# Attention with rotary embedding and a gated block: transposes whose result nobody reads, kept only ahead of the first rotary sum

## Chip, cores and metric

One core of a Trainium2 chip runs the whole program. The metric is device time in microseconds (us) of one execution, the median over several. The engines are TensorE (PE, with its weight loads PEld beside it), VectorE (DVE), ScalarE (ACT), GpSimd (POOL) and SyncE (SP), which issues DMAs. The matrix results of PE go to PSUM banks, from which DVE and ACT read.

## What is computed

Eight batches of eight heads, 576 positions, head width 64. Queries and keys are rotated, attention is computed, and the heads of one batch together (512 wide) go through a causal convolution of five taps, a sigmoid gate and two 512 x 512 products:

```python
q_rot, k_rot = rotate(q), rotate(k)
scores = (1 / sqrt(D)) * q_rot @ k_rot.T
attn = exp(scores - max(scores)); attn /= sum(attn) + 1e-9
x = heads side by side of (attn @ v)          # B, S, 512
gate = sigmoid(sum over k of conv_w[k] * x shifted by k)
out = (gate * (x @ w_val)) @ w_out
```

## The kernel before

Work goes in 32 pairs of heads (`p`), four pairs to a batch. For a pair the queries fall into four chunks of 128 positions and a fifth that holds the last 64 positions of both heads. The steps that matter here, with their lines:

- `rope_mul`, `rope_add` (L283, L287) rotate; for pair 0 alone `rope_mm` (L294) makes the rotary sum on PE. `qk_hi`, `qk_lo` (L303 to L314) split each value into a high and a low part.
- `s_mm` (L339), a **score chunk**: 12 matmuls for the two heads of a chunk (6 for the fifth), each head into a score bank `ps_s`. There are two such banks.
- `s_max` (L345), the **row maximum**, on DVE; `s_exp` (L353), the exp, on ACT, which also hands over the row sums (the READ_ACCUMULATOR rows). Only then is the score bank free for the next chunk.
- `t_mm` (L400, L365), a **turn**: PE transposes the exp results into banks `ps_t`, of which there are four; `t_copy` (L438, L440) copies them to SBUF.
- `pv_mm`, `pv_left` (L449, L459) multiply with the values; `x_norm` (L506) divides by the sums, `tap` (L532) and `gate` follow.
- `f_mm` (L572): the two 512-wide products of a batch, in 24 groups of matmuls for each stage, between the pairs of the next batch. Until 96 us there is none of this work yet to put between.

Every engine takes its instructions in the order in which the program issues them. That order is not found by rules: the string `ORDER` lists all jobs one by one, with the buffers that each takes, and `Plan.run` walks through it. A second table, `FILLS`, maps a position in this list to a pair of numbers (count, bank). When the walk comes to such a position, `fill` (L356) first issues that many transposes of the identity matrix into the `ps_t` bank named, ahead of the job. Nothing reads what they write:

```python
def fill(n, slot):
    bank = psum.tile([128, 512], F32, name="ps_t", tag=f"ps_t{slot}")
    for _ in range(n):
        T.transpose(out=bank[:, 0:128], in_=ident, identity=ident)
```

They read only `ident`, but they take a `ps_t` bank like any job, so they wait for whoever had it last, and the next job that takes it stands behind them. They appear in the trace as L360. The first group of 34, at position 11, stands ahead of `rope_mm`, while PE has no data. The next ten stand at these places: 21, 26 and 11 transposes between the score chunks and turns of pair 0; 7 ahead of the fifth chunk of pair 1; 2 ahead of the second chunk of pair 2; 5 between pairs 2 and 3; 13 between pairs 3 and 4 and 3 behind the first chunk of pair 4; 3 and 7 around the fifth chunk of a later pair, at 137 and 139 us.

Of the kernel before, what the change touches and what calls it, by code (L numbers as in the profile page):

```python
# [161 lines left out]
3252 3268 3261 3253 3262 3275 3254:2 3284:2 3250 3255 3285 3256 3276 3286 3277V:0 3289:1 3278 3287A:2 3290 3294:0 3291 3304:3 3292V:1 3295 3293 3299:2  # L162
3288 3300 3301 3296 3302V:0 3305 3303 3297A:1 3306 3298 3307A:2 3308
"""
FILLS = {11: (34, 0), 46: (21, 0), 63: (26, 2), 90: (11, 3), 176: (7, 0), 207: (2, 2), 277: (5, 1), 360: (13, 2), 372: (3, 3), 647: (3, 3), 660: (7, 2)}


class Plan:
# [16 lines left out]
    def run(self, engine, fill, behind):  # L185
# [10 lines left out]
        for step, entry in enumerate(ORDER.split()):  # L196
# [4 lines left out]
            writer.update(dict.fromkeys(w, i))  # L201
            if step in FILLS:
                fill(*FILLS[step])
            self.slots = [int(x) for x in slots]
# [691 lines left out]
```

## Time and profile before

| what | before |
|---|---|
| median of three runs | 674.58 us (674.34 to 674.8) |
| the profiled execution: its time | 675.45 us |
| its span, first to last instruction | 673.7 us |
| mean granted PE clock in it | 0.997 |
| DVE busy, ACT busy, POOL busy | 553.5 (82%), 514.2 (76%), 288.9 us (43%) |
| L360 MATMUL, the filling transposes | 132, 270 to 477 ns each |

Busy time is the time in which an engine had at least one instruction under way; matmuls overlap, so a group's elapsed time is shorter than the sum of its instructions. In the page's rows of slices each digit is the busy share of a fortieth of the span in tenths, and PEclk is the clock that PE was granted, in tenths of full speed. In a row such as `x12 [1.41 <-ACT p L353]` the bracket gives the idle time of the engine just ahead of it and what ended it. Times in timelines count from the start of the span.

### The profile page before, as it was taken

To read this page: it belongs to the slowest core of one execution; us is meant where nothing else is said; L and a number is where in the kernel's file an instruction comes from. 1 tells how busy PE (TensorE), PEld (TensorE's weight loads), DVE (VectorE), ACT (ScalarE), POOL (GpSimd) and SP (SyncE) were. 2 spreads that over 40 slices of the span, in tenths; PEclk is the share of its full clock that TensorE was granted. 3 is DMA by queue.
4 is the path that set the end of the run, shared out by engine and by line. 5 is a ranking of instruction groups with operands and counts; after the bars stand their busy time and mean duration, and the time that the engine had idled before them with its cause. 6 is when DMAs were issued, how large, how long until landed. Compare 5 with 4: busy or idle time off the path is not lost. (4 is left out here: it accounts for less than half of the span.)

```text
span 673.7 us, 18254 instructions
## 1 busy us (share of the span) xinstructions
PE 658.8 (98%) x7224; PEld 534.8 (79%) x7224; DVE 553.5 (82%) x932; ACT 514.2 (76%) x1251; POOL 288.9 (43%) x258
## 2 busy tenths in 40 slices
PE   8889899999999999999999999999999999999998
PEld 7666677778788778887877888877788878787887
DVE  5999899999788888988787988987878889887732
ACT  3989888888887868887777887787778777776722
POOL 0445334423645622253554335456546563353122
PEclk9999899999999999999999999999999999999999
DMA  6435324523422534232434323343433144301112
GB/s 205 141 120 162 118 79 141 170 84 98 152 84 91 165 100 135 75 112 84 139 90 140 105 77 113 96 133 108 134 123 97 47 134 126 99 28 48 35 55 72
DMA packets 46743, 72.66 MB, mean 108 GB/s; under 512 B 15897, under 2 KB 25666, under 8 KB 46658
## 3 DMA queue, kind: packets, MB, share of 16 engines
q1 hardware_dynamic: 46114, 70.91, 34.0%
q8 instruction: 57, 0.93, 0.6%
q10 hardware_dynamic: 544, 0.59, 0.3%
q14 instruction: 28, 0.23, 0.1%
HBM read 61.89 MB, written 9.59 MB: 106 GB/s over the span
## 5 line engine op out<-in xcount | busy, mean ns | idle before, releaser
L345 DVE TENSOR_REDUCE nm<-ps_s 128x1 f32<-128x576 f32 x288 | 207.4, 752 | 58.8 <-PE ps_s L339 56.8
L353 ACT ACTIVATE p<-ps_s,nm 128x576 f32<-128x576 f32 x288 | 213.1, 744 | 54.4 <-DVE nm L345 50.3
L339 PE MATMUL ps_s<-k,q 64*128 64x288 f32 (+1 forms) x1728 | 175.9, 308 | 6.2 <-ACT p L353 5.9
L339 PEld LDWEIGHTS ps_s<-k,q 64*128 64x128 f32 (+1 forms) x1728 | 138.3, 185 | 33.7 <-ACT p L353 19.5
L438 ACT COPY pt<-ps_t 128x512 f32<-128x512 f32 (+1 forms) x241 | 126.7, 547 | 48.2 <-PE ps_t L400 47.2
L449 PE MATMUL ps_a<-pt,v 128*64 128x320 f32 (+1 forms) x1024 | 137.8, 412 | 0.9 <-ACT pt L438 0.4
L400 PEld LDWEIGHTS ps_t<-ident,p 64*128 64x128 f32 x2428 | 99.2, 138 | 21.3 <-issue 8.4
L400 PE MATMUL ps_t<-ident,p 64*128 64x64 f32 x2428 | 110.9, 226 | 1.7 <-ACT pr L438 0.5
L532 DVE SCALAR_TENSOR_TENSOR g<-x,cw,g 128x576 f32<-128x576 f32 (+1 forms) x132 | 108.8, 829 | 2.0 <-ACT g L529 1.5
L572 PE MATMUL ps_f<-y,wout_hi 128*128 128x288 f32 (+2 forms) x512 | 107.1, 302 | 0.4 <-DVE o L596 0.4
L449 PEld LDWEIGHTS ps_a<-pt,v 128*64 128x64 f32 x1024 | 68.0, 136 | 45.8 <-issue 3.1
L572 PEld LDWEIGHTS ps_f<-y,wout_hi 128*128 128x128 f32 x512 | 81.3, 188 | 6.0 <-ACT pt L438 2.1
L283 POOL TENSOR_TENSOR qin<-qin,tab 128x640 f32<-128x640 f32 x39 | 60.3, 1559 | 43.2 <-DVE kin L287 16.6
L572 PE MATMUL ps_f<-xh,wval_hi 128*128 128x288 f32 (+2 forms) x256 | 78.2, 309 | 0.6 <-ACT pt L438 0.3
L572 PE MATMUL ps_f<-xh,wval_lo 128*128 128x288 f32 (+2 forms) x256 | 75.4, 298 | 0.0
L572 PE MATMUL ps_f<-xl,wval_hi 128*128 128x288 f32 (+2 forms) x256 | 75.1, 295 | 0.0
L283 POOL TENSOR_TENSOR kin<-kin,tab 128x576 f32<-128x576 f32 x31 | 43.8, 1418 | 71.2 <-DVE g L532 41.6
L572 PE MATMUL ps_f<-y,wout_lo 128*128 128x288 f32 (+2 forms) x256 | 74.2, 295 | 0.0
L587 POOL TENSOR_TENSOR y<-y,y 128x288 fp32r<-128x288 f32 (+2 forms) x64 | 51.1, 806 | 51.4 <-ACT y L584 23.1
L519 POOL TENSOR_TENSOR xl<-x,xh 128x576 fp32r<-128x576 f32 (+2 forms) x33 | 46.3, 1406 | 55.4 <-ACT xh L513 23.6
L353 ACT ACTIVATION_READ_ACCUMULATOR p<-ps_s,nm 128x1 f32 x288 | 57.5, 200 | 0.0
L572 PEld LDWEIGHTS ps_f<-xh,wval_hi 128*128 128x128 f32 x256 | 47.9, 188 | 7.2 <-ACT pt L438 4.9
(90 smaller groups left out, 841.5 us busy)
## 6 DMA issues: line engine op xcount, KB each, us to landing
kin<-in_k SPq DMA_DIRECT2D x31, 576.0 KB
qin<-in_q SPq DMA_DIRECT2D x31, 512.0 KB
v<-in_v SPq DMA_DIRECT2D x32, 320.0 KB
out_t<-o SPq DMA_DIRECT2D x56, 144.0 KB
rb<-rd SPq DMA_DIRECT2D x31, 144.0 KB
rb<-rd SPq DMA_DIRECT2D x31, 128.0 KB
wst<-in_w_val SPq DMA_DIRECT2D x4, 512.0 KB
wst<-in_w_out SPq DMA_DIRECT2D x4, 512.0 KB
```

The costliest lines, as they stand in the source:

```text
L283: return eng.tensor_tensor(out=t[:, i, a:b], in0=t[:, 0 if p < RAW else i, a:b], in1=table[:, i, a:b], op=ALU.mult)
L339: T.matmul(out=tiles[h][:, half, 0:288], lhsT=st["q"][rows, x, c * 128:c * 128 + 128], rhs=st["k"][rows, y, k0:k0 + 288], start=(i == 0), ...
L345: V.tensor_reduce(out=st[f"nm{i}"], in_=st[f"s{i}"], axis=AX.XY, op=ALU.max, negate=True)
L353: A.activation(out=st[f"p{t}"][:, part].rearrange("p (b x) -> p b x", b=2), in_=st[f"s{i}"], func=AF.Exp, bias=st[f"nm{i}"], scale=1.0, ac ...
L400: T.transpose(out=st["b" + key + x][:, k * D:(k + 1) * D], in_=src[rows], identity=ident[rows, rows])
L438: A.copy(out=dst, in_=src)
L449: T.matmul(out=st[f"a{g}"][HEAD[h], 0:n], lhsT=st["v"][:, j, h, :], rhs=st[f"pt{g}"][:, h * 4 + j], start=(j == 0), stop=False)
L519: return G.tensor_tensor(out=st["xl"][:, a:b], in0=xs[p % 2][:, 4 + a:4 + b], in1=st["xh"][:, a:b].bitcast(F32), op=ALU.subtract)
L532: return V.scalar_tensor_tensor(out=g, in0=x_sb[:, a + k:b + k], scalar=w, in1=g, op0=ALU.mult, op1=ALU.add)
L572: T.matmul(out=acc[:, 0:n], lhsT=wt[w][:, kc, ds], rhs=mv, start=(kc == 0 and i == 0), stop=(kc == NCH - 1 and i == 2))
L587: return G.tensor_tensor(out=ffn[b][1][:, dc, lo:hi], in0=ffn[b, "y", dc, lo], in1=ffn[b][0][:, dc, lo:hi].bitcast(F32), op=ALU.subtract)
```

## The change

The table `FILLS` keeps its first entry alone:

```diff
-FILLS = {11: (34, 0), 46: (21, 0), 63: (26, 2), 90: (11, 3), 176: (7, 0), 207: (2, 2), 277: (5, 1), 360: (13, 2), 372: (3, 3), 647: (3, 3), 660: (7, 2)}
+FILLS = {11: (34, 0)}
```

So ten groups with 98 transposes are no longer issued. Nothing is computed differently, and no job changes its place. Three places on PE follow, with the waits that each instruction carries (`PE_49`, `Activation_49` and so on are the semaphores of the engine waited for; `x10` counts equal rows).

PE in pair 0, from the end of the first score chunk on, before:

```order
L360 MATMUL ps_t<-ident 128x128 x21
L339 MATMUL ps_s<-k_71,q_73 128x288 [waits Activation_49] x2
L339 MATMUL ps_s<-k_71,q_73 128x288 x10
L400 MATMUL ps_t<-ident,p 128x64 [waits PE_49]
L400 MATMUL ps_t<-ident,p 128x64 x15
L360 MATMUL ps_t<-ident 128x128 x26
L339 MATMUL ps_s<-k_71,q_73 128x288 [waits Activation_49] x2
```

The same place with the change:

```order
L339 MATMUL ps_s<-k_71,q_73 128x288 [waits Activation_49] x2
L339 MATMUL ps_s<-k_71,q_73 128x288 x10
L400 MATMUL ps_t<-ident,p 128x64 x16
L339 MATMUL ps_s<-k_71,q_73 128x288 [waits Activation_49] x2
L339 MATMUL ps_s<-k_71,q_73 128x288 x2
```

The two groups are gone, and with them the turn's wait for PE's own last write into the bank that the first group had taken. The score chunks keep their two waits for ACT.

PE where pair 3 ends and pair 4 begins (the turn of pair 3, a group of 13, the first score chunk of pair 4), before:

```order
L400 MATMUL ps_t<-ident,p 128x64 x14
L360 MATMUL ps_t<-ident 128x128 [waits DVE_49]
L360 MATMUL ps_t<-ident 128x128 x12
L339 MATMUL ps_s<-k_71,q_73 128x288
L339 MATMUL ps_s<-k_71,q_73 128x288 [waits PE_49,Activation_49]
L339 MATMUL ps_s<-k_71,q_73 128x288 [waits Pool_49]
```

With the change:

```order
L400 MATMUL ps_t<-ident,p 128x64 x14
L339 MATMUL ps_s<-k_71,q_73 128x288
L339 MATMUL ps_s<-k_71,q_73 128x288 [waits PE_49,Activation_49]
L339 MATMUL ps_s<-k_71,q_73 128x288 [waits Pool_49]
L339 MATMUL ps_s<-k_71,q_73 128x288 x9
```

The group and its wait for DVE are gone; the chunk keeps its waits for ACT and POOL.

PE at the last two groups, of 3 and 7, before:

```order
L360 MATMUL ps_t<-ident 128x128 [waits DVE_49]
L360 MATMUL ps_t<-ident 128x128 x2
L400 MATMUL ps_t<-ident,p 128x64 [waits PE_49]
L400 MATMUL ps_t<-ident,p 128x64 [waits DVE_49]
L400 MATMUL ps_t<-ident,p 128x64 x14
L339 MATMUL ps_s<-k_71,q_73 128x288 [waits Activation_49]
L339 MATMUL ps_s<-k_71,q_73 128x288 x5
L360 MATMUL ps_t<-ident 128x128 [waits Activation_49]
L360 MATMUL ps_t<-ident 128x128 x6
L400 MATMUL ps_t<-ident,p 128x64 [waits PE_49]
L400 MATMUL ps_t<-ident,p 128x64 [waits Activation_49]
```

With the change:

```order
L400 MATMUL ps_t<-ident,p 128x64 [waits DVE_49] x2
L400 MATMUL ps_t<-ident,p 128x64 x14
L339 MATMUL ps_s<-k_71,q_73 128x288 [waits Activation_49]
L339 MATMUL ps_s<-k_71,q_73 128x288 x5
L400 MATMUL ps_t<-ident,p 128x64 [waits Activation_49] x2
```

The waits for DVE and ACT that the groups carried pass on to the turns, whose two banks each wait now for the engine that read them last.

## The prediction

> **What bounds the kernel now.** I read the page first, then three stretches of the span, then the clock window by window.
>
> ```profile
> PE 658.8 (98%) x7224; PEld 534.8 (79%) x7224; DVE 553.5 (82%) x932; ACT 514.2 (76%) x1251; POOL 288.9 (43%) x258
> ...
> PEclk9999899999999999999999999999999999999999
> ```
>
> ```profile
> 45.00:75.00 30.00, 27.37 (x308) 18.15 (x305) 29.67 (x46) 27.91 (x71) 13.30 (x11) 1.00 0.51 164
> 75.00:96.00 21.00, 18.82 (x215) 14.36 (x215) 18.43 (x29) 16.28 (x39) 8.96 (x7) 0.92 0.33 100
> 96.00:670.00 574.00, 571.75 (x6297) 470.02 (x6297) 470.07 (x791) 437.71 (x1066) 253.00 (x225) 1.00 0.33 102
> ```
>
> In the whole-span shares TensorE (PE) is the bound. The stretches (columns: from:to and length, then busy time and count of PE, PEld, DVE, ACT, POOL, then granted clock, DMA share, GB/s) show where. From 96 us on PE is busy 571.75 of 574 us: whatever is late at 96 us is late at the end. Before that PE has holes, 2.63 us of 30 from 45 to 75, while VectorE (DVE) is full there, 29.67 of 30. So the start is a loop: scores on PE, row maximum on DVE, exp on ScalarE (ACT), next scores. Eight of the ten removed groups lie in it, the last two at 137 and 139 us.
>
> The PEclk line has a single 8, in its fifth slice (67 to 84 us), and the stretch 75 to 96 a mean clock of 0.92. Finer windows find it, and the PE timeline (start, length, what ran) shows what stood there:
>
> ```profile
> 17.91:21.32 3.41, 3.41 (x44) 3.02 (x42) 3.34 (x7) 3.26 (x8) 0.99 (x2) 1.00 0.22 81
> 21.32:24.73 3.41, 2.35 (x21) 1.76 (x20) 3.41 (x6) 2.99 (x8) 1.26 (x2) 1.00 0.47 166
> 75.93:79.35 3.42, 1.91 (x28) 1.53 (x29) 3.01 (x7) 2.40 (x6) 1.56 (x1) 1.00 0.37 103
> 79.35:82.76 3.41, 3.41 (x29) 3.25 (x25) 3.25 (x4) 3.41 (x8) 2.00 (x2) 0.50 0.01 2
> 82.76:86.17 3.41, 3.19 (x38) 2.37 (x38) 2.38 (x5) 2.08 (x5) 0.00 (x0) 1.00 0.54 173
> ```
>
> ```profile
> 77.99 1.05 PE L339 MATMUL ps_s<-k,q 128*128 128x288 f32 x6 [1.41 <-ACT p L353]
> ...
> 80.08 2.92 PE L360 MATMUL ps_t<-ident 128*128 128x128 f32 x13
> 82.94 1.06 PE L339 MATMUL ps_s<-k,q 64*128 64x288 f32 x12
> ```
>
> The clock is 0.50 for exactly one window of 3.41 us, 79.35 to 82.76, and 1.00 on both sides. The window ahead of it had PE busy only 1.91 us, so 1.51 idle; its longest hole is the 1.41 us before 77.99. The window 21.32 to 24.73, busy 2.35, so 1.06 idle, was followed by no drop. So **somewhere between 1.06 and 1.51 us of idle in a window of 3.41 us the clock falls for the next window**. Inside the slow window PE ran the rest of a turn and then the 13 filling transposes at (82.94 - 80.08) / 13 = 0.22 us each, and after it the clock was back: transposes alone brought it back. The Trainium skill, page "TensorE: Matmul & The Clock Gate", Part 4: PE-mode transpose, says that transposes do not count as activity for the full clock. By that the removed groups protect nothing and the sum would be zero, 674.6 us; this trace disagrees, with those 13 at half clock and 1.00 from 82.76.
>
> **The change part by part.** 98 transposes go: 21, 26, 11, 7, 2, 5, 13, 3, 3 and 7. Nothing else changes place on any engine. First, what each group delayed. Pair 0:
>
> ```profile
> 12.33 2.51 PE L360 MATMUL ps_t<-ident 128*128 128x128 f32 x21
> 14.77 1.11 PE L339 MATMUL ps_s<-k,q 64*128 64x288 f32 x12
> ...
> 16.31 3.06 PE L360 MATMUL ps_t<-ident 128*128 128x128 f32 x26
> 19.30 1.24 PE L339 MATMUL ps_s<-k,q 64*128 64x288 f32 x11
> ...
> 23.97 1.42 PE L360 MATMUL ps_t<-ident 128*128 128x128 f32 x11
> 25.76 1.07 PE L339 MATMUL ps_s<-k,q 128*128 128x288 f32 x6 [0.36 <-ACT p L353]
> ```
>
> ```profile
> 13.87 0.19 ACT L353 ACTIVATION_READ_ACCUMULATOR p<-ps_s,nm 128x1 f32 x1
> ...
> 14.59 0.20 ACT L353 ACTIVATION_READ_ACCUMULATOR p<-ps_s,nm 128x1 f32 x1
> ...
> 18.06 0.19 ACT L353 ACTIVATION_READ_ACCUMULATOR p<-ps_s,nm 128x1 f32 x1
> ...
> 19.36 0.19 ACT L353 ACTIVATION_READ_ACCUMULATOR p<-ps_s,nm 128x1 f32 x1
> ...
> 25.51 0.19 ACT L353 ACTIVATION_READ_ACCUMULATOR p<-ps_s,nm 128x1 f32 x1
> ```
>
> A score chunk needs two score banks, and each is free when the exp that reads it has handed over its sum (the READ_ACCUMULATOR row). For the chunk at 14.77 these end at 14.06 and 14.79, for that at 19.30 at 18.25 and 19.55, and for the one-bank chunk at 25.76 at 25.70. Groups 1 to 3 (21, 26, 11) ended inside waits that remain: **they give back nothing**. The chunk at 19.30 even took 1.24 us instead of 1.06, since its second bank came 0.3 us late. The same holds further on:
>
> ```profile
> 41.93 0.98 PE L360 MATMUL ps_t<-ident 128*128 128x128 f32 x7
> 43.17 1.05 PE L339 MATMUL ps_s<-k,q 128*128 128x288 f32 x6 [0.26 <-ACT p L353]
> ...
> 62.44 0.76 PE L360 MATMUL ps_t<-ident 128*128 128x128 f32 x5
> ```
>
> ```profile
> 63.40 0.19 ACT L353 ACTIVATION_READ_ACCUMULATOR p<-ps_s,nm 128x1 f32 x1
> ```
>
> ```profile
> 137.18 0.55 PE L360 MATMUL ps_t<-ident 128*128 128x128 f32 x3
> 137.78 0.80 PE L400 MATMUL ps_t<-ident,p 64*128 64x64 f32 x16
> ...
> 139.41 0.93 PE L360 MATMUL ps_t<-ident 128*128 128x128 f32 x7
> 140.40 0.71 PE L400 MATMUL ps_t<-ident,p 64*128 64x64 f32 x16
> ```
>
> ```profile
> 137.41 0.41 DVE L506 TENSOR_TENSOR x<-ps_a,rb 128x256 f32<-128x256 f32 x1
> ```
>
> ```profile
> 140.31 0.23 ACT L353 ACTIVATION_READ_ACCUMULATOR p<-ps_s,nm 128x1 f32 x1
> ```
>
> Group 4 (7 at 41.93) is followed by a wait for exp anyway. Group 6 (5 at 62.44) covers time until the exp bank of 63.59. Group 9 (3 at 137.18) is followed by a turn that needs the bank which the DVE frees at 137.82; group 10 (7 at 139.41) by a turn whose second half needs the exp sum of 140.54, so both turns end where they did. Groups 5 and 8 (2 and 3 transposes) are too short to matter at (14.77 - 12.33) / 21 = 0.116 us each; I cost them at nothing.
>
> Group 7 alone was in the way, because it ran in the slow window:
>
> ```profile
> 81.46 0.19 ACT L353 ACTIVATION_READ_ACCUMULATOR p<-ps_s,nm 128x1 f32 x1
> ```
>
> ```profile
> 84.04 0.76 DVE L345 TENSOR_REDUCE nm<-ps_s 128x1 f32<-128x576 f32 x1 [1.02 <-PE ps_s L339]
> ```
>
> Its score chunk needed the exp sum of 81.65 and began at 82.94, and the DVE idled 1.02 us before 84.04. Full gain if nothing else changes: 1.0 us. But without it the window 79.35 to 82.76 has a hole from 80.08 to 81.65, 1.57 us, which by the rule above keeps the clock at half through 86.17, and then costs up to what a half-speed window can cost a busy PE, 3.41 / 2 = 1.7 us: chunk 0.5 earlier, later work 1.5 later. Bounds -1.0 to +1.0; I take **0**, the middle, since the two rows pull equally.
>
> Second, the price of a slow clock. Transposes went from 0.116 to 0.22 us, a factor of 1.9. No score chunk ran slow in this trace; of the 1.06 us of a chunk 0.29 is the length of its last matmul (the median below, columns min/median/max in ns), and I let only the rest stretch, so the estimate is (1.06 - 0.29) x 0.9 = **0.7 us** for a slow chunk. Bounds: 0, where the DVE is late anyway, and 1.7 for a window full of PE work.
>
> ```profile
> L339 PE MATMUL ps_s<-k,q x266: 286/292/402, 11.7 to 98.5; 64*128 64x288 f32 x118, 128*128 128x288 f32 x15
> ```
>
> Third, where windows go slow. I let the grid of 3.41 us stand as in this trace. Pair 0 now has holes from 12.33 to 14.1, 16.31 to 18.3, 18.6 to 19.6 and 24.0 to 25.76.
>
> ```profile
> 16.63 0.75 DVE L345 TENSOR_REDUCE nm<-ps_s 128x1 f32<-128x576 f32 x1
> ...
> 20.59 1.42 DVE L345 TENSOR_REDUCE nm<-ps_s 128x1 f32<-128x576 f32 x2
> ...
> 26.93 0.76 DVE L345 TENSOR_REDUCE nm<-ps_s 128x1 f32<-128x576 f32 x1
> ```
>
> - 11.08 to 14.49: hole of 1.77 less a matmul's edge, over 1.51, so 14.49 to 17.91 is slow. The chunk at 14.84 ends 0.7 later, 16.6; its maximum began at 16.63 with the DVE at other work until then. Free.
> - 14.49 to 17.91: PE busy with the chunk to 16.6 and with the turns that took 15.88 to 16.31, now about 0.8, to 17.4: 0.9 idle, so the clock returns. 17.91 to 21.32: holes of 0.4 and 1.0, 1.4 together, undecided. 21.32 to 24.73: the 1.06 of before and 0.7 of group 3, 1.76, if it was not slow already.
> - So one of the two windows 21.32 to 24.73 and 24.73 to 28.14 is slow. In the first lies the chunk before group 3, in the second the chunk of 25.76, whose maximum follows at 26.93; either is on the loop with no slack, as the maximum at 20.59 shows behind the chunk that ended at 20.54: +0.7. The hole of group 3 then slows the turns and sums after it: another +0.7, taken as one more chunk's worth. Pair 0: **+1.4**, from 0 (all on slack) to +2.1 (three chunks). Another phase of the grid changes which chunk pays, not whether a window over 1.51 is found: the holes of pair 0 sum to 6.5 us in 13.4.
>
> Later, group 4 leaves 1.24 us of hole, group 6 about 1.1, groups 9 and 10 together about 1.35 in one window of 3.41: each inside the undecided band. I take one of the three: **+0.7**; bounds 0 and 0.7 + 0.7 + 1.7 = 3.1, the last because PE is full after 140 us.
>
> Sum: 1.4 + 0.7 + 0 = +2.1 us. The profiled execution took 675.45 us (span 673.7 and 1.75 around it), so 677.55; it stood 0.87 above the median of the three runs, 674.58, so the forecast for the median is **676.7 us**. Bounds: 0 + 0 - 1.0 = -1.0 and 2.1 + 3.1 + 1.0 = +6.2, that is 673.6 to 680.8.
>
> **The rivals.**
> A. The clock does not fall in the holes, or only where the DVE has slack: for it, one window with 1.06 us idle stayed fast, and the first slow window would be free; against it, the window before 79.35, with less idle than pair 0 will have. Time: 674.6, within 0.2% at any rate. The Trainium skill, page "TensorE: Matmul & The Clock Gate", section "Why this matters for your kernels", warns only of idle gaps over about 3 us, one whole idle window; no hole here reaches that in one piece, so its time would be this one. The trace differs: 1.41 us in one piece was enough at 79.35.
> B. Faster: the fills themselves held scores back. The mechanism is group 7, 13 transposes at 0.22 us ahead of a chunk that was ready 1.2 us earlier: -1.0 (the DVE's idle time there), and -1.7 if moved holes also spare the slow window itself (3.41 / 2), so 672.9 to 673.6. It decides if a window with 1.6 us of hole leaves the clock as it is. Against it: the other nine groups end in waits that remain.
> C. Heavier: half clock holds over several windows in pair 0, and groups 9 and 10 add a slow window where PE is full: +4 to +6.2, 678.6 to 680.8. For it: PE's holes in pair 0 are half of its time. Against it: at half clock PE needs twice the time, so the holes close and the clock returns after one window, as at 82.76.
>
> **How the numbers follow.** Forecast (+1.35 to +4) 0.50, A 0.25, B 0.10, C 0.15. A difference of 0.2%, 1.35 us, is about what a measurement of this kernel can tell from no change. Slower: 0.50 + 0.15 = 0.65; of B 0.07 lies below 673.2, so faster 0.07 and same 0.28. The range is that of the bounds, 673.6 to 680.8: it leaves out B, 0.10, and next to nothing of C.
>
> **What would show it.** Right: windows at 0.50 clock between 14 and 28 us, score chunks of 1.7 to 1.8 us in them, DVE idle before the maxima of pair 0 longer by 1 to 2 us, the chunks after groups 1 to 3 starting on their exp sums, not earlier. Group 7's chunk starts near 81.7 plus the shift. PE from 96 us on as full as now. Wrong: clock 1.00 in the windows after the holes; or slow windows and yet the same start of the work that PE does at 96 us, which would mean slack that I do not see.

## The result and the profile after

The changed kernel takes 679.72 us in the median of six executions (679.18 to 682.52), against 674.69 us for the kernel before, measured beside it: a ratio of 1.0087, 95% interval 1.0073 to 1.0101. So it is slower by 5.0 us, where +2.1 was forecast. The profiled execution is one of the two long ones: 682.52 us, span 680.7. One execution of the kernel before in a later round, 877 us at a mean clock of 0.65, is left out of every comparison.

The page of the changed kernel, in the two rows that the prediction showed of before:

```profile
PE 657.5 (97%) x7126; PEld 532.2 (78%) x7126; DVE 551.8 (81%) x932; ACT 513.3 (75%) x1251; POOL 288.6 (42%) x258
...
PEclk9698869999999999999999999999999999999999
```

PE has less to do and takes longer; the PEclk row, with a single 8 before, now has a 6, two 8s and another 6 in its first six slices. The windows of the clock in the changed kernel (from:to and length, busy time of PE, PEld, DVE, ACT, POOL, granted clock, DMA share, GB/s), on the grid of this execution (the clock changes only at the ends of windows of 3.41 us, and where that grid lies differs from one execution to the next):

```profile
14.29:17.70 3.41, 1.94 (x28) 1.59 (x28) 3.41 (x9) 2.35 (x6) 0.00 (x0) 1.00 0.98 339
17.70:21.12 3.42, 0.87 (x3) 0.55 (x5) 3.42 (x8) 2.45 (x6) 1.40 (x1) 0.50 0.70 243
21.12:24.53 3.41, 3.40 (x30) 2.78 (x30) 2.72 (x5) 2.58 (x6) 1.42 (x1) 0.50 0.08 17
24.53:27.94 3.41, 1.54 (x14) 1.13 (x14) 3.41 (x7) 2.91 (x9) 1.53 (x1) 1.00 0.70 232
27.94:31.36 3.42, 3.41 (x40) 2.98 (x40) 2.50 (x5) 2.55 (x6) 1.41 (x1) 0.50 0.20 78
...
45.01:48.42 3.41, 2.05 (x23) 1.65 (x23) 3.40 (x7) 3.20 (x7) 1.42 (x1) 1.00 0.58 186
48.42:51.83 3.41, 3.02 (x27) 2.71 (x29) 2.65 (x6) 2.04 (x8) 1.73 (x2) 0.50 0.71 240
51.83:55.25 3.42, 3.42 (x20) 1.72 (x18) 2.44 (x4) 2.78 (x8) 0.81 (x1) 0.50 0.01 2
...
65.49:68.90 3.41, 1.91 (x24) 1.51 (x23) 3.39 (x5) 3.35 (x9) 3.11 (x3) 1.00 0.77 202
68.90:72.32 3.42, 3.41 (x29) 2.92 (x31) 2.84 (x5) 2.53 (x7) 1.74 (x2) 0.50 0.61 220
...
82.56:85.97 3.41, 1.89 (x29) 1.52 (x31) 3.01 (x6) 2.46 (x6) 1.55 (x1) 1.00 0.39 107
85.97:89.38 3.41, 2.16 (x25) 1.84 (x23) 3.25 (x4) 3.41 (x8) 1.99 (x2) 0.50 0.01 2
89.38:92.80 3.42, 3.00 (x24) 2.10 (x24) 2.88 (x6) 2.42 (x8) 0.00 (x0) 0.50 0.61 179
92.80:96.21 3.41, 3.41 (x20) 2.03 (x18) 1.58 (x3) 1.96 (x7) 1.40 (x1) 0.50 0.58 164
96.21:677.00 580.79, 577.29 (x6390) 474.02 (x6387) 475.13 (x801) 442.13 (x1077) 256.68 (x227) 1.00 0.33 101
```

Nine windows run at half clock in five places: behind group 1's hole, behind group 3's, behind group 4's, behind group 6's and, three in a row, where the kernel before had its one. From 96 us on the clock is 1.00 and PE nearly as full as before, idle for 3.5 of 580.8 us against 2.3 of 574. Where the time goes is seen when the same work is found in both timelines. PE in the kernel before (start, length, what ran):

```profile
29.80 1.04 PE L339 MATMUL ps_s<-k,q 64*128 64x288 f32 x12
...
49.60 1.25 PE L339 MATMUL ps_s<-k,q 64*128 64x288 f32 x12
...
67.07 1.06 PE L339 MATMUL ps_s<-k,q 64*128 64x288 f32 x12
...
90.76 1.14 PE L339 MATMUL ps_s<-k,q 64*128 64x288 f32 x12
...
138.51 1.06 PE L339 MATMUL ps_s<-k,q 128*128 128x288 f32 x6
```

PE in the changed kernel:

```profile
1.36 6.89 PE L360 MATMUL ps_t<-ident 128*128 128x128 f32 x34 [1.36 <-POOL ident masks.py:199]
...
16.09 1.05 PE L339 MATMUL ps_s<-k,q 64*128 64x288 f32 x11 [0.33 <-ACT p L353]
...
20.85 1.81 PE L339 MATMUL ps_s<-k,q 64*128 64x288 f32 x11 [0.69 <-ACT p L353]
...
24.86 1.05 PE L339 MATMUL ps_s<-k,q 64*128 64x288 f32 x11 [0.16 <-ACT p L353]
27.63 1.57 PE L339 MATMUL ps_s<-k,q 128*128 128x288 f32 x6 [1.71 <-ACT p L353]
29.13 1.97 PE L400 MATMUL ps_t<-ident,p 64*128 64x64 f32 x32
...
32.62 1.04 PE L339 MATMUL ps_s<-k,q 64*128 64x288 f32 x12
...
45.98 1.05 PE L339 MATMUL ps_s<-k,q 128*128 128x288 f32 x6 [1.17 <-ACT p L353]
...
54.80 1.25 PE L339 MATMUL ps_s<-k,q 64*128 64x288 f32 x12
...
68.91 1.81 PE L339 MATMUL ps_s<-k,q 64*128 64x288 f32 x11 [0.95 <-ACT p L353]
...
73.65 1.06 PE L339 MATMUL ps_s<-k,q 64*128 64x288 f32 x12
...
84.55 1.06 PE L339 MATMUL ps_s<-k,q 128*128 128x288 f32 x6 [1.41 <-ACT p L353]
...
98.90 1.26 PE L339 MATMUL ps_s<-k,q 64*128 64x288 f32 x12
...
146.77 1.06 PE L339 MATMUL ps_s<-k,q 128*128 128x288 f32 x6
```

| place | before starts | after starts | later by | added |
|---|---|---|---|---|
| first chunk of pair 1 | 29.80 | 32.62 | 2.82 | 2.82 (1.25 of it at the start) |
| fifth chunk of pair 1 | 43.17 | 45.98 | 2.81 | 0.0 |
| second chunk of pair 2 | 49.60 | 54.80 | 5.20 | 2.4, group 4 |
| second chunk of pair 3 | 67.07 | 73.65 | 6.58 | 1.4, group 6 |
| fifth chunk of pair 3 | 77.99 | 84.55 | 6.56 | 0.0 |
| third chunk of pair 4 | 90.76 | 98.90 | 8.14 | 1.6, groups 7 and 8 |
| between groups 9 and 10 | 138.51 | 146.77 | 8.26 | 0.1 |
| end of the span | 673.7 | 680.7 | 7.0 | -1.3 |

The 1.25 us at the start have nothing to do with the change: the group of 34 that both kernels keep took 6.89 us here and 5.32 in the profile of before, because the clock came up at 7.46 us and not at 4.25, and the first score chunk starts at 12.60 us and not at 11.35. Less that, pair 0 cost 1.6 us. A chunk that runs slow takes 1.81 us (row 20.85), the same at full clock 1.05 (row 16.09), so 0.76 each.

Of the 1.3 us that come back late, most lies at one place, a rotary sum on DVE, before and after:

```profile
310.17 1.98 DVE L287 TENSOR_TENSOR kin<-kin 128x576 f32<-128x576 f32 x1
```

```profile
317.90 0.91 DVE L287 TENSOR_TENSOR kin<-kin 128x576 f32<-128x576 f32 x1
```

It runs beside a POOL multiplication of 3.1 us in both (308.45 to 311.53 before, 315.14 to 318.21 with the change), so for 1.4 us of the sum's time before and for 0.3 us after. That this overlap is the cause was not tried.

### The profile page after: what moved, and what is told of

Its sections match the earlier page's. It is cut to its first block, busy times and chain, and to the rows that moved or that the text cites. A ratio compares the mean times of both kernels' runs of the same rounds, so it can differ in the third digit from the quotient of the medians.

```text
span 680.7 us, 18059 instructions
## 1 busy us (share of the span) xinstructions
PE 657.5 (97%) x7126; PEld 532.2 (78%) x7126; DVE 551.8 (81%) x932; ACT 513.3 (75%) x1251; POOL 288.6 (42%) x258
## 5 line engine op out<-in xcount | busy, mean ns | idle before, releaser
L339 PE MATMUL ps_s<-k,q 64*128 64x288 f32 (+1 forms) x1728 | 181.0, 314 | 14.3 <-ACT p L353 14.2
L339 PEld LDWEIGHTS ps_s<-k,q 64*128 64x128 f32 (+1 forms) x1728 | 142.3, 190 | 42.9 <-ACT p L353 28.4
L449 PE MATMUL ps_a<-pt,v 128*64 128x320 f32 (+1 forms) x1024 | 141.9, 421 | 0.7 <-DVE o L596 0.4
L400 PEld LDWEIGHTS ps_t<-ident,p 64*128 64x128 f32 x2428 | 101.8, 141 | 22.2 <-issue 8.7
L400 PE MATMUL ps_t<-ident,p 64*128 64x64 f32 x2428 | 113.4, 229 | 2.7 <-DVE x L506 1.0
L449 PEld LDWEIGHTS ps_a<-pt,v 128*64 128x64 f32 x1024 | 69.7, 140 | 47.4 <-issue 6.0
L440 DVE COPY pt<-ps_t 128x512 f32<-128x512 f32 (+1 forms) x79 | 49.1, 623 | 5.6 <-PE ps_t L400 5.5
```

What stands on the lines that cost most here:

```text
L339: T.matmul(out=tiles[h][:, half, 0:288], lhsT=st["q"][rows, x, c * 128:c * 128 + 128], rhs=st["k"][rows, y, k0:k0 + 288], start=(i == 0), ...
L400: T.transpose(out=st["b" + key + x][:, k * D:(k + 1) * D], in_=src[rows], identity=ident[rows, rows])
L440: V.tensor_copy(out=dst, in_=src)
L449: T.matmul(out=st[f"a{g}"][HEAD[h], 0:n], lhsT=st["v"][:, j, h, :], rhs=st[f"pt{g}"][:, h * 4 + j], start=(j == 0), stop=False)
```

## The experiments

Theories. **Clock**: the empty holes lower PE's clock, and the time is that of the slow windows. **Waits**: the banks and waits that went with the groups matter, not their work. **Draw**: the executions of the first measurement happened to have an unlucky position of the grid. The number of slow windows in an execution follows, rounded, from its mean clock: (1 - clock) x span / (0.5 x 3.41).

### One transpose in each group

```diff
-FILLS = {11: (34, 0)}
+FILLS = {11: (34, 0), 46: (1, 0), 63: (1, 2), 90: (1, 3), 176: (1, 0), 207: (1, 2), 277: (1, 1), 360: (1, 2), 372: (1, 3), 647: (1, 3), 660: (1, 2)}
```

> All ten groups are back, each with a single transpose: the same banks are taken and the same waits stand in the rows as before the change, but PE's holes stay empty. Clock theory (the holes cool PE): 679 to 680 us, slow windows in pair 0, at the fifth chunk of pair 1 and ahead of pairs 3 and 4, mean clock near 0.977. Rival theory (the waits and bank order that went with the groups matter, not their work): 674.7 us and a mean clock of 0.997.

Measured: 677.93 us (676.66 to 681.61), ratio to before 1.0056 (1.0034 to 1.0078); mean clock 0.977 to 0.987 in its executions, 5 to 9 slow windows. The banks and waits are those of before, and most of the loss stays, 3.7 of the 5.0 us (674.26 for the kernel before beside it): the rival falls as the main cause. That it is under 679 is a miss of the number; what the missing 1.3 us are was not separated. Its windows of pair 0:

```profile
14.89:18.30 3.41, 3.07 (x28) 2.65 (x28) 3.41 (x8) 1.56 (x5) 1.37 (x1) 0.50 0.96 340
18.30:21.71 3.41, 2.65 (x24) 2.34 (x26) 2.73 (x6) 2.94 (x7) 1.01 (x2) 0.50 0.10 37
21.71:25.13 3.42, 3.29 (x24) 2.45 (x20) 3.05 (x5) 2.99 (x8) 0.68 (x2) 0.50 0.52 172
25.13:28.54 3.41, 2.10 (x9) 1.53 (x7) 2.48 (x5) 2.23 (x6) 1.76 (x2) 0.50 0.46 154
28.54:31.95 3.41, 3.40 (x40) 2.64 (x41) 2.49 (x6) 2.31 (x6) 1.16 (x2) 0.50 0.00 0
```

All five are slow, with PE idle for 0.34, 0.76, 0.13, 1.31 and 0.01 us. None reaches the 1.51 us that let the clock fall in the kernel before, and yet the clock did not return until one was full. Behind the third it stayed down with 0.13 us idle.

### The groups of pair 0 alone, and the later ones alone

```diff
-FILLS = {11: (34, 0)}
+FILLS = {11: (34, 0), 46: (21, 0), 63: (26, 2), 90: (11, 3)}
```

> The three groups of pair 0 (21, 26, 11) are kept, the seven later ones left out. In the profiles the maxima of pair 0 end 1.6 us later with the change than without, those from pair 1 to pair 4 another 5.4 us, of which about 1.2 us is won back after 157 us. Clock theory: 679.7 - 1.6 = 678.1 us, no slow window ahead of 40 us. If the loss came from pair 0 alone: 674.7 us.

```diff
-FILLS = {11: (34, 0)}
+FILLS = {11: (34, 0), 176: (7, 0), 207: (2, 2), 277: (5, 1), 360: (13, 2), 372: (3, 3), 647: (3, 3), 660: (7, 2)}
```

> The three groups of pair 0 are left out, the seven later ones kept. Clock theory: 674.7 + 1.6 = 676.3 us, slow windows between 14 and 32 us and the one ahead of pair 4 that the kernel before has. If the later groups do not matter: 679.7 us.

Measured: with pair 0's groups alone 678.78 us, ratio 1.0064 (1.0043 to 1.0084), 3 to 7 slow windows; in its profile the first slow window starts at 79.1 us. With the later groups alone 676.93 us, ratio 1.0027 (1.0012 to 1.0042), 3 to 6 slow windows, in its profile five in a row from 16.1 to 33.2 us and none ahead of pair 4 (1.31 us idle in the window at 80.97, clock held), which the expectation had. Both are about 0.6 us above their expectations. Both sets matter, the later one more, as the table above says. The two losses, 4.5 and 2.7 us, sum to 7.2 and not to 5.0: a place that is late meets another part of the grid, and the two were not measured on one grid. How they combine stays open.

### An eleventh group

To the table of before:

```diff
-360: (13, 2),
+346: (6, 0), 360: (13, 2),
```

> All ten groups as before the change and an eleventh of 6 transposes ahead of the fifth chunk of pair 3, in the hole of 1.41 us that preceded the one slow window of the kernel before. Clock theory: that window (1.51 us idle of 3.41) has then about 0.8 us idle, the clock stays at 1.00 and the 13 transposes behind it take 1.5 us instead of 2.9: 1.0 us faster than before, 673.7 us. If transposes do not hold the clock, or that slow window costs nothing: 674.7 us.

Measured: 673.88 us (672.97 to 674.8), ratio 0.9984 (0.9968 to 1.0000). Nine of ten executions have a mean clock of 1.000; of 31 executions of the kernel before beside it nine had 0.999 or 1.000 (median 673.12 us), thirteen one slow window (674.26) and nine two (676.21). PE around the new group:

```profile
78.25 0.88 PE L360 MATMUL ps_t<-ident 128*128 128x128 f32 x6 [0.68 <-ACT pt L438]
78.98 1.05 PE L339 MATMUL ps_s<-k,q 128*128 128x288 f32 x6
...
80.78 1.64 PE L360 MATMUL ps_t<-ident 128*128 128x128 f32 x13
82.35 1.27 PE L339 MATMUL ps_s<-k,q 64*128 64x288 f32 x11
```

The six transposes run 0.88 us in the hole, the 13 behind them 1.64 us where the kernel before needed 2.92 at half clock. Transposes do hold the clock. The gain is smaller than a slow window's price: the nine executions at 1.000 have a median of 673.86 us, 0.7 above those of the kernel before without a slow window. Why was not tried.

### Group 7, groups 9 and 10, and group 4, each left out alone

From the table of before, in this order:

```diff
-360: (13, 2)
```

> Only the group of 13 between pairs 3 and 4 is left out. The prediction's term: 0, from -1.0 (the chunk behind it starts 1.2 us earlier) to +1.0. Theory of an uneven gate (the clock falls behind a window with 1.36 to 1.41 us idle or more, and returns only behind a window with next to no idle time): the slow window that the kernel before mostly has at 79 us is then followed by one or two more, each worth 1 to 1.7 us: +1.5 to +2.5, 676 to 677 us, mean clock 0.990 to 0.992.

```diff
-647: (3, 3), 660: (7, 2)
```

> Only the last two groups, of 3 and 7 at 137 and 139 us, are left out. The profile of the changed kernel has the clock at 1.00 there and no shift: 674.3 us, mean clock as before (0.995 to 1.000). The prediction's upper price, a slow window where PE is full: 676.0 us.

```diff
-176: (7, 0)
```

> Only the group of 7 ahead of the fifth chunk of pair 1 is left out. In the profile of the changed kernel two slow windows followed its hole (1.17 us and some edges, 1.37 us idle in the window) and the maxima behind it ended 2.4 us later. Uneven gate: 1.5 to 2.4 us slower, 676 to 676.7, in those executions whose grid puts all the idle time into one window, and no loss in the others, so a wide spread. The prediction's price for such a place, one slow chunk: +0.7, 675.0 us.

Measured: without group 7, 675.36 us, ratio 1.0008 (0.9994 to 1.0021); without groups 9 and 10, 674.64, ratio 0.9999 (0.9985 to 1.0013); without group 4, 675.63, ratio 1.0020 (1.0006 to 1.0035).

Groups 9 and 10 are worth nothing, as expected. Group 7 alone is not the 1.5 to 2.5 us of the expectation, a miss: ten of its twelve executions have two slow windows, two have three. Its profile shows the pair:

```profile
79.28:82.70 3.42, 2.31 (x25) 1.99 (x27) 3.17 (x4) 3.42 (x8) 2.05 (x3) 0.50 0.01 3
82.70:86.11 3.41, 3.35 (x27) 2.42 (x27) 2.86 (x6) 1.91 (x5) 0.00 (x0) 0.50 0.54 173
```

The hole that the 13 leave (2.31 us busy) keeps the clock down for one window more; then PE is full and it returns. In the changed kernel group 8 is gone as well, and the window there had 0.42 us idle (row 89.38), and a third slow one followed. Group 4, +1.2 us by the medians, lies between its two expectations. In its profile three slow windows follow:

```profile
39.69:43.10 3.41, 2.06 (x31) 1.59 (x28) 2.79 (x6) 3.20 (x8) 1.33 (x2) 1.00 0.51 166
43.10:46.51 3.41, 3.04 (x23) 2.60 (x23) 2.64 (x5) 2.53 (x7) 1.42 (x1) 0.50 0.54 171
46.51:49.93 3.42, 3.04 (x28) 2.57 (x29) 2.66 (x6) 2.05 (x7) 1.73 (x2) 0.50 0.46 168
49.93:53.34 3.41, 3.41 (x18) 1.69 (x14) 2.58 (x4) 2.92 (x8) 0.66 (x1) 0.50 0.00 0
```

Here 1.35 us idle let the clock fall. Two of its twelve executions have one slow window (674.01 us), seven two (675.54), three three (676.87).

### Half of each group, and half with the eleventh

```diff
-FILLS = {11: (34, 0)}
+FILLS = {11: (34, 0), 46: (11, 0), 63: (13, 2), 90: (6, 3), 176: (4, 0), 207: (1, 2), 277: (3, 1), 360: (7, 2), 372: (2, 3), 647: (2, 3), 660: (4, 2)}
```

> All ten groups at half their length (11, 13, 6, 4, 1, 3, 7, 2, 2, 4). If the loss goes with the length of the holes: half of it, 2.5 us, 676.8 us. If there is a threshold at 1.36 to 1.41 us idle in a window: most holes stay below it, only that of pair 0 ahead of the third chunk (about 1.45 us) reaches it in some executions: 674.3 to 675.5 us, mean clock mostly as before.

The second version adds `346: (6, 0)` to these.

> All ten groups at half length and the eleventh group of 6 ahead of the fifth chunk of pair 3. Threshold theory: no window of the start reaches 1.36 us idle except by a rare position of the grid, so the mean clock is 1.000 in nearly all executions, and the time is that of the executions of the kernel before that show no slow window (673.1 to 673.6 us): 673.4 us, about 1 us under the kernel before. If the full groups were needed: 674.2 us or more and slow windows.

Measured: half of the transposes lose nothing: 674.19 us, ratio 0.9988 (0.9976 to 1.0000). Two windows in pair 0 of its profile:

```profile
19.66:23.08 3.42, 2.20 (x30) 1.80 (x30) 3.35 (x6) 3.21 (x8) 1.41 (x1) 1.00 0.00 0
23.08:26.49 3.41, 2.17 (x19) 1.65 (x19) 3.41 (x6) 2.90 (x9) 1.53 (x1) 1.00 0.73 234
```

They have 1.22 and 1.24 us idle and the clock stays at 1.00. This execution is one of three at a mean clock of 1.000; five of the twelve have two or three slow windows, so half the length does not hold the clock on every grid. With the eleventh group the median is 673.23 us (672.85 to 674.28), ratio 0.9985 (0.9973 to 0.9997), nine of twelve executions without a slow window: faster than both kernels, by about 1 us against before.

### The changed kernel again

> The changed kernel once more, for the spread over positions of the grid. Uneven gate: mean clock between 0.976 and 0.980 (8 to 10 slow windows) in each execution, 679 to 682.5 us, and the more slow windows the longer. If its first measurement was an unlucky draw of the grid: executions with 3 to 5 slow windows and 677 us among them.

Measured, with no edit: 679.49 us, ratio 1.0097 (1.0066 to 1.0127). Three of four executions have 8 slow windows (679.1 to 679.6 us), one has 12 (683.63), more than expected. The first measurement was no unlucky draw.

## Why the prediction came out as it did

- **The groups gave back nothing** and the chunks behind them kept their waits: right. The second chunk of pair 0 ends at 16.09 + 1.05 = 17.14 against 15.88, later by the start's 1.25 and not earlier.
- **Transposes hold the clock**: right, shown by the single transposes (loss stays) and by the eleventh group (gain). The Trainium skill, page "TensorE: Matmul & The Clock Gate", Part 4: PE-mode transpose, has it the other way, from bf16 transposes; these are f32, and for them the runs decide.
- **The clock falls between 1.06 and 1.51 us of idle time in a window**: right, and narrower now: it fell behind 1.35 (row 39.69 without group 4) and stayed behind 1.24 (row 23.08 at half length). In a few windows it held with up to 1.43 (last section). Rival A is out. The Trainium skill, page "TensorE: Matmul & The Clock Gate", section "Why this matters for your kernels", warns of idle gaps over about 3 us; here shorter ones were enough, as the longest single hole ahead of the slow windows at 48.42 us was 1.17.
- **A slow chunk costs 0.7**: right, 0.76.
- **Pair 0, +1.4**: near in size, 1.6 in the profile (2.7 on another set of grids), but partly by luck: the third chunk (row 20.85), which the prediction left at full clock, ran slow, the chunk ahead of group 3 (row 24.86) did not, and the fifth chunk and the turns behind it (rows 27.63 and 29.13) did.
- **"0.9 idle, so the clock returns"**: this is the step that failed. I used the threshold for falling also for returning. Slow windows with 0.13 to 1.31 us idle were followed by another slow one (the first four above, and the rows 48.42, 85.97 and 89.38 of the changed kernel); only windows that were all but full brought the clock back. So a place mostly costs two or three windows, not one chunk.
- **Later holes, +0.7 for one of three**: mis-sized, and this is most of what the sum lacks. Two of the three fell, groups 4 and 6, with 2.4 and 1.4 us in the profile; groups 9 and 10 cost nothing, as their window stayed at 1.00. Group 4 had two slow windows, by the step above. Group 6 had one alone, and the price for it was wrong as well: its chunk (row 68.91) lost 0.76, but PE was busy for 3.41 us in that window (row 68.90), and the work behind the chunk ran slow too.
- **Group 7, 0**: alone it is inside its bounds (0.9 us by the medians, not distinguishable from zero); together with group 8's loss, 1.6. Rival B, that this group stood in the way, did not decide: with the group the chunk waited, without it the clock stayed down.
- **Rival C** named what happened, half clock over several windows, and its range, +4 to +6.2, holds the measured +5.0. But it put the windows into pair 0, where 1.6 us arose, against 5.4 behind it. The argument against it, that the holes close at half clock, was wrong: PE still waits for DVE and ACT between the chunks, long enough to miss a full window. Its second half, a slow window at groups 9 and 10, did not come.
- **The range, 673.6 to 680.8**: it holds 679.72, though the forecast of +2.1 is less than half of the measured +5.0. That is luck in part: the upper bound counted 1.7 us for a slow window at groups 9 and 10 that did not come, and it made room for the slow windows that the sum lacks.

## What to carry to other kernels

Where PE waits for other engines, look at its idle time per window of 3.41 us, not at single holes: here about 1.4 us in one window was mostly enough to lose the clock, and then PE had to be all but full for a whole window to get it back. Work that nobody reads, put into such holes, paid where it ended inside the wait; half of it was enough for the median here, and a place that had none was worth up to another 1 us. Count slow windows from the mean clock of every execution before comparing medians, since where the grid falls differs from one to the next.

## What the runs showed of the hardware

The gate of PE's clock is uneven: it closes and opens by different measures. Over twelve profiles, and apart from their first and last microseconds, the clock fell behind windows with 1.35 us of PE idle time and more and held with up to 1.31 (three times with 1.41 to 1.43). But a slow window with as little as 0.12 us was followed by another slow one, and none with more than 0.22 brought the clock back. In the first microseconds, where PE ran the 34 transposes alone, the clock came up behind windows with up to 0.58 us idle. The bands of falling and holding overlap by some hundredths, so idle time is not quite what is counted. The grid of 3.41 us has another offset in each execution: the clock first came up between 4.2 and 7.5 us. For the kernel before that is a spread from 672.8 to 677.5 us with 0 to 2 slow windows, far wider than the 674.3 to 675.0 of its first six executions.
